# Earlier loads, one rounding step on ScalarE and a read-out with priority in a three-stage kernel (gated linear attention, softplus layer, routed experts)

## The chip, the cores and the metric

The kernel runs on one core of a Trainium2 chip. The metric is device time in microseconds (us) of one launch; the time shown for the kernel before is the median of 3 runs. One more execution was taken by the hardware profiler; its trace gives the rows below. Engines are called as in the profile: PE is TensorE (PEld its weight loads), DVE is VectorE, ACT is ScalarE, POOL is GpSimd, SP is the queue of SyncE that issues most transfers.

## The reference, cut to what matters

```
# attention: 4 batches, 8 heads, 768 positions, width 48
f = 1 / (1 + exp(-f_logit))
state = f[t][:, None] * state + outer(k[t], v[t]);  y[t] = q[t] @ state
x = y laid out as 3072 tokens of 384
# layer: w_in 384 x 2048, w_out 2048 x 384
h = x @ w_in;  g = max(h, 0) + log1p(exp(-abs(h)));  x2 = g @ w_out
# experts: 8, one per token (argmax), w1 384 x 1024, w2 1024 x 384
logits = x2 @ w_gate + modality_bias[modality_id];  e = argmax(logits)
out = softmax(logits)[e] * (max(x2 @ w1[e], 0) @ w2[e])
```

w_in and w_out come as 64-bit floats and are turned into 32-bit ones on the chip.

## The kernel before, in words

**Attention** is cut into 32 units (two heads, 384 positions each). A unit u has loads f, k, q, v (`att_load`), a preparation on ACT and DVE (`att_prep1`, `att_prep2`: 1 + exp(-f), a running product by a scan, its inverse, scaled keys and queries), transposes, products and masks on PE and DVE, and an output y on ACT (`att_out`) that SP copies into `xf` (`xf<-y`, 2 or 3 transfers per unit). Four units make one group of 384 tokens. Units 0 to 3 have a start of their own, `start_load` and `start_units`, where PE, DVE and ACT follow an order written out by hand (`manual_schedule`) and two units share one tile, so that pair 0 holds units 0 and 1 and pair 1 units 2 and 3. Every other order is the planner's: it takes the instructions of an engine by readiness and by a priority that falls in the order of the program.

**Layer.** For 8 groups G and 16 blocks i of 128 hidden columns, step s = 16 G + i does `up` (h in PSUM), softplus and `down` (adds into three PSUM tiles `x2ps`, one per 128 tokens). In group 0 (`softplus` with `lean`) the weights are 32-bit and are decoded while the steps run: `raw(n)` is a tile of 768 KB of raw words, even n for input weights, odd n for output weights; `scale_hi` is one ACT instruction on it, `decode` three DVE instructions (L461, L464, L465). From step 16 on each product is made of three (xh with wih, xl with wih, xh with wil; and so for w_out). For steps 16 to 111 two steps share one softplus, `pair` (48 of them): ACT makes exp (L626) and log (L627), DVE the rounding term w = ((e + 1) - 1) - e (L628, L629), the sum (L630), and after ACT's high part (L631) the low part (L632, L633).

**Read-out and routing.** After the last `down` of a group, `route1(G, j)` reads tile j of `x2ps` for the logits (L667) and the rows (ACT L672 for j = 0 and 2, DVE L670 for j = 1). The next group's first `down` writes the same three tiles, so it waits for them. `route2` picks the expert and POOL scatters the rows (L714). After the last group the experts run over slots of 256 or 128 tokens.

**Order at the start.** SP loads f and k of pair 0, f of pair 1, q of pair 0, two v, then the rest, then raw(0), raw(1), raw(2) and unit 4. f, k, q of unit 5 and raw(3) are held behind `marks["out"]`, the last transfer of unit 3's output (`follow`; `load_out(1)` with `first_out`). `NWARM` = 12 products with the identity run on PE in the start (L326) and 12 more at step 1 (L902); nothing reads their result.

Of the kernel before, what the change touches and what calls it, by code (L numbers as in the profile page):

```python
# [32 lines left out]
NWARM = 12  # L33
# [15 lines left out]
def moe_chain(ctx, tc, qT, kT, fT, vp, w_in, w_out, mod, w_gate, mbias, w1, w2, out):  # L49
# [40 lines left out]
    def att_load(u):  # L90
        d = units[u] = {}
        for nm, src in (("f", fT), ("k", kT), ("q", qT)):
            t = ap2.tile([128, TG], F32, tag=nm, name=nm, bufs=2 if nm == "f" else 3)
            ins = nc.sync.dma_start(t, src[u])
            if u == 5:
                follow(ins, marks["out"])
            d[nm] = t
        v = ap2.tile([128, 3 * 96], F32, tag="v", name="v", bufs=4)
        nc.sync.dma_start(v, vp[u])
        d["v"] = v  # L100
# [134 lines left out]
    def start_load():  # L235

        words = wih_raw.rearrange("p a b -> p (a b)").bitcast(F32)
        pair = [{nm: words[:, 768 * (4 * x + n):768 * (4 * x + n) + 768].rearrange("p (j t) -> p j t", j=2)
                 for n, nm in enumerate(("f", "k", "q", "F0"))} for x in range(2)]
        for u in range(4):  # L240
            units[u] = {nm: t[:, u % 2, :] for nm, t in pair[u // 2].items()}
        units["pairs"] = pair

        def get(nm, src, x):
            for j in range(2):
                nc.sync.dma_start(pair[x][nm][:, j, :], src[2 * x + j])

        def get_v(u):
            units[u]["v"] = ap2.tile([128, 3 * 96], F32, tag="v", name="v", bufs=4)
            nc.sync.dma_start(units[u]["v"], vp[u])  # L250

        get("f", fT, 0)
        get("k", kT, 0)
        get("f", fT, 1)
        get("q", qT, 0)
        get_v(0)
        get_v(1)
        get("k", kT, 1)
        get("q", qT, 1)
        get_v(2)  # L260
        get_v(3)

    def start_units():

        pair = units.pop("pairs")
        vec, act, pe = nc.vector, nc.scalar, nc.tensor
        h01 = [ps_h.tile([128, TG], F32, tag="h", name="h") for _ in range(2)]
        zu = x2ps[2]

        def scan(u):  # L270
            f = units[u]["f"]
            vec.tensor_tensor_scan(f, f, clampt.to_broadcast([128, TG]), 1.0, op0=ALU.mult, op1=ALU.min)

        def one_plus(u):
            f = units[u]["f"]
            act.activation(f, f, AF.Exp, scale=-1.0)
            act.activation(f, f, AF.Copy, bias=1.0)

        def keys(x):
            p = pair[x]  # L280
            vec.tensor_copy(fl[:, 2 * x:2 * x + 2], p["f"][:, :, TG - 1])
            vec.tensor_tensor(p["k"], p["k"], p["f"], op=ALU.mult)

        def inverse(x):
            p = pair[x]
            act.activation(p["F0"], p["f"], AF.Ln)
            act.activation(p["F0"], p["F0"], AF.Exp, scale=-1.0)

        def queries(x):
            p = pair[x]  # L290
            vec.tensor_tensor(p["f"], p["f"], p["F0"], op=ALU.mult)
            vec.scalar_tensor_tensor(p["F0"], p["f"], 2.0, p["F0"], op0=ALU.subtract, op1=ALU.mult)
            vec.tensor_tensor(p["q"], p["q"], p["F0"], op=ALU.mult)

        def sums(u):
            o = 144 * (u % 2)
            kt, v = units[u].pop("kt"), units[u]["v"]
            for c in range(3):
                for x in ([0, 2], [1, 2], [2])[c]:
                    for h in range(2):  # L300
                        vh = v[:, 96 * c + 48 * h:96 * c + 48 * h + 48]
                        n = 1
                        if x == 0:
                            n, vh = 2, vh.unsqueeze(1).to_broadcast([128, 2, 48])
                        pe.matmul(zu[64 * h:64 * h + 64, o + 48 * x:o + 48 * x + 48 * n], kt[:, c, 64 * h:64 * h + 64], vh,
                                  start=(u % 2 == 0 and c == 0 and x == 0), stop=True, skip_group_check=True)

        def states(u):
            o = 144 * (u % 2)
            for h in range(2):  # L310
                r, e = slice(64 * h, 64 * h + 64), slice(64 * h, 64 * h + D)
                act.copy(sts[u][r, 0:3, e], zu[r, o:o + 144].rearrange("p (c e) -> p c e", c=3))

        with tc.manual_schedule(engines={mybir.EngineType.PE, mybir.EngineType.DVE, mybir.EngineType.Activation}):
            for u in range(4):
                one_plus(u)
            scan(0)
            scan(1)
            keys(0)
            inverse(0)  # L320
            att_T(0)
            att_T(1)
            scan(2)
            scan(3)
            for _ in range(NWARM):
                pe.matmul(x2ps[0][:, 0:128], ident, ident, start=True, stop=True)  # L326
            inverse(1)
            sums(0)
            sums(1)
            queries(0)  # L330
            keys(1)
            att_A(0, h01)
            att_A(1, x2ps)
            states(0)
            states(1)
            att_T(2)
            att_T(3)
            queries(1)
            ya = ps_r.tile([128, 512], F32, tag="r", name="r")
            pa2 = [ps_r.tile([128, 512], F32, tag="r", name="r") for _ in range(2)]  # L340
            att_qS(0, ya)
            sums(2)
            sums(3)
            states(2)
            states(3)
            att_mask(0, h01)
            att_A(2, pa2)
            att_AV(0, ya)
            att_mask(1, x2ps)
            scale_hi(raw(0, 3))  # L350
            att_A(3, h01)
            att_out(0, ya)
            att_Y(1, x2ps[0])
            att_mask(2, pa2)
            att_out(1, x2ps[0])
            att_Y(2, x2ps[1])
            att_mask(3, h01)
            load_in(0, True)
            att_out(2, x2ps[1])
            scale_hi(raw(1, 2))  # L360
            yd = ps_r.tile([128, 512], F32, tag="r", name="r")
            att_Y(3, yd)
            att_out(3, yd)
            scale_hi(raw(2, 3))
        for u in range(4):
            units.pop(u)
# [100 lines left out]
    def raw(n, k):  # L467
        c = 1536 * (n % 4)
        return flat[n // 4 % 2][:, c:c + 1536].rearrange("p (k f) -> p k f", k=k)
# [148 lines left out]
    def pair(s):  # L618

        d = gst[s]  # L620
        e, r = d.pop("e"), d.pop("r")
        w = pp.tile([128, 2, TG], F32, tag="w2", name="w2", bufs=1)
        g = pp.tile([128, 2, TG], F32, tag="l2", name="l2", bufs=1)
        hi = pp.tile([128, 2, TG], F32R, tag="hi2", name="hi2")
        lo = pp.tile([128, 2, TG], F32R, tag="lo2", name="lo2")
        nc.scalar.activation(e, e, AF.Exp, scale=-1.0)  # L626
        nc.scalar.activation(g, e, AF.Ln, bias=1.0)  # L627
        nc.vector.tensor_scalar(w, e, 1.0, -1.0, op0=ALU.add, op1=ALU.add)  # L628
        nc.vector.tensor_tensor(w, w, e, op=ALU.subtract)  # L629
        nc.vector.tensor_tensor(g, r, g, op=ALU.add)  # L630
        nc.scalar.copy(hi, g)  # L631
        nc.vector.tensor_tensor(g, g, hi.bitcast(F32), op=ALU.subtract)  # L632
        nc.vector.tensor_tensor(lo, g, w, op=ALU.subtract)  # L633
        for j in range(2):
            gst[s + j]["hi"], gst[s + j]["lo"] = hi[:, j, :], lo[:, j, :]
# [27 lines left out]
    def route1(G, j):  # L663
        if j == 0:
            rt[G] = {"lg": sm("lg", [128, 3, 8]), "rows": gp.tile([128, 3, RW], F32, tag="rows", name="rows", bufs=1)}
        lg, rows = rt[G]["lg"], rt[G]["rows"]
        nc.vector.scalar_tensor_tensor(lg[:, j, :], x2ps[j][:, DM:DM + 8], 1.0 / WS, biasT[:, 3 * G + j, :],  # L667
                                       op0=ALU.mult, op1=ALU.add)
        if j == 1:
            nc.vector.tensor_scalar(rows[:, j, 0:DM], x2ps[j][:, 0:DM], 1.0 / WS, None, op0=ALU.mult)  # L670
        else:
            nc.scalar.activation(rows[:, j, 0:DM], x2ps[j][:, 0:DM], AF.Copy, scale=1.0 / WS)  # L672
# [169 lines left out]
    nc.sync.dma_start(raw(0, 3), src_in(0))  # L842
    nc.sync.dma_start(raw(1, 2), src_out(0))
    nc.sync.dma_start(raw(2, 3), src_in(1))
    att_load(4)
    late_consts()
    start_units()
    first_out = marks["out"]
    first_mask = marks["mask"]
    att_load(5)  # L850
    load_out(0, True)
    make_wp(0)
    load_in(1, True)

    at(0, lambda: load_out(1))
    at(5, pad_out)
    at(10, make_bias)
    for m in range(1, NF // 2):
# [433 lines left out]
```

## Time and profile before

| | |
|---|---|
| median of 3 runs | 841.43 us (839.96 to 841.88) |
| the profiled execution | 838.99 us |
| its span, first to last instruction | 837.2 us |
| PE busy in it | 801.8 us (96%) |
| DVE busy | 647.1 us (77%) |
| ACT busy | 536.5 us (64%) |

The profiled execution's own time is 1.8 us above its span; that part lies ahead of and behind the instructions. It stands 2.4 us under the median of the runs. Busy shares are means over stages with different limits, and ends of matmuls are modelled, so a busy PE is not PE at its peak.

### The profile page before, as it was taken

The page shows a single profiled execution, that of the slowest core. Times are in us where ns is not written, and L with a number is a line of the kernel's source. Part 1 is how long each engine was busy: PE and PEld are TensorE (multiplying, and loading weights), DVE is VectorE, ACT ScalarE, POOL GpSimd, SP SyncE. Part 2 cuts the span into 40 slices and gives each one's busy share as a digit, 9 for nine tenths or more (in the row PEclk, how much of TensorE's full clock was granted, in tenths as well). Part 3 has the DMA queues.
Part 4 walks back from the last instruction along what each step waited for, and adds up shares of the span by engine and source line. Part 5 has one row for each costly group of instructions (what it writes and reads, how often), then busy time and mean ns, then how long its engine had stood idle before and what let it go on. Part 6 is the DMA issues. An engine that isn't in the chain of part 4 may idle for free. (4 is left out here: it accounts for less than half of the span.)

```text
span 837.2 us, 15948 instructions
## 1 busy us (share of the span) xinstructions
PE 801.8 (96%) x5815; PEld 742.9 (89%) x5815; DVE 647.1 (77%) x1275; ACT 536.5 (64%) x1074; POOL 63.2 (8%) x79
## 2 busy tenths in 40 slices
PE   6799999999999999999999999999999999999995
PEld 5556668999999999899999999999999999999995
DVE  6899999988888888878887877888966666554441
ACT  6678787767667666667666665566756555555441
POOL 2000000200000010010010010101111110111100
PEclk9999999999999999999999999999999999999998
DMA  8685221321122132121221010199987667775590
GB/s 277 215 302 178 67 69 43 95 63 52 56 81 58 47 92 60 44 90 52 59 73 43 16 36 8 53 332 357 301 272 229 207 195 219 223 251 191 187 325 15
DMA packets 58522, 115.83 MB, mean 138 GB/s; under 512 B 7719, under 2 KB 33114, under 8 KB 58432
## 3 DMA queue, kind: packets, MB, share of 16 engines
q1 hardware_dynamic: 54144, 104.76, 39.4%
q0 software_dynamic: 3328, 9.49, 3.0%
q8 instruction: 49, 0.80, 0.4%
q10 hardware_dynamic: 960, 0.44, 0.2%
q14 instruction: 41, 0.34, 0.1%
HBM read 92.11 MB, written 18.62 MB: 132 GB/s over the span
## 5 line engine op out<-in xcount | busy, mean ns | idle before, releaser
L646 PE MATMUL x2ps<-woh,hi 128*128 128x392 f32 x336 | 115.5, 344 | 3.9 <-DVE rows L670 2.2
L566 PE MATMUL h<-xh,wih 128*128 128x384 f32 x336 | 118.1, 351 | 1.1 <-DVE e L580 0.7
L566 PE MATMUL h<-xl,wih 128*128 128x384 f32 x336 | 112.6, 335 | 2.2 <-DVE xl L393 2.2
L646 PE MATMUL x2ps<-woh,lo 128*128 128x392 f32 x336 | 114.3, 341 | 0.4 <-DVE lo L606 0.4
L646 PE MATMUL x2ps<-wol,hi 128*128 128x392 f32 x336 | 114.6, 341 | 0.0
L566 PE MATMUL h<-xh,wil 128*128 128x384 f32 x336 | 113.2, 337 | 0.0
L993 PE MATMUL h<-thl,w1h 128*128 128x256 f32 x576 | 106.5, 285 | 1.7 <-DVE hl L996 1.5
L993 PEld LDWEIGHTS h<-thl,w1h 128*128 128x128 f32 x576 | 89.2, 189 | 3.1 <-DVE hl L996 2.3
L955 DVE TENSOR_TENSOR w2l<-raw,w2h 128x768 fp32r<-128x768 f32 x64 | 60.7, 950 | 33.4 <-ACT w2h L954 33.1
L955 DVE TENSOR_TENSOR w1l<-raw,w1h 128x768 fp32r<-128x768 f32 x48 | 45.8, 954 | 48.7 <-ACT w1h L954 45.7
L993 PE MATMUL h<-thl,w1l 128*128 128x256 f32 x288 | 80.4, 281 | 0.0
L631 ACT CAST hi<-l 128x768 fp32r<-128x768 f32 x48 | 40.0, 834 | 62.0 <-DVE l L630 50.8
L1016 PE MATMUL x2ps<-w2h,hh 128*128 128x384 f32 x224 | 76.4, 341 | 0.0
L1016 PE MATMUL x2ps<-w2l,hh 128*128 128x384 f32 x224 | 75.1, 335 | 0.0
L954 ACT CAST w1h<-raw 128x768 fp32r<-128x768 f32 x48 | 40.1, 836 | 54.2 <-DMA raw<-in_w_dram 51.0
L1016 PE MATMUL x2ps<-w2h,hl 128*128 128x384 f32 x224 | 74.8, 336 | 0.0
L646 PEld LDWEIGHTS x2ps<-woh,hi 128*128 128x128 f32 x336 | 63.0, 188 | 6.4 <-DVE rows L670 3.5
L714 POOL DMA_INDIRECT xs<-rows,pos x24 | 26.7, 1111 | 552.9 <-ACT r L616 180.3
L566 PEld LDWEIGHTS h<-xh,wih 128*128 128x128 f32 x336 | 63.0, 188 | 5.4 <-DVE e L580 1.5
L566 PEld LDWEIGHTS h<-xl,wih 128*128 128x128 f32 x336 | 63.1, 188 | 3.5 <-DVE xl L393 3.5
L646 PEld LDWEIGHTS x2ps<-woh,lo 128*128 128x128 f32 x336 | 63.1, 188 | 1.1 <-DVE lo L606 1.0
L646 PEld LDWEIGHTS x2ps<-wol,hi 128*128 128x128 f32 x336 | 63.1, 188 | 0.0
(242 smaller groups left out, 1841.6 us busy)
## 6 DMA issues: line engine op xcount, KB each, us to landing
raw<-in_w_dram SPq DMA_DIRECT2D x112, 384.0 KB, 5.4
xs<-padt SPq DMA_DIRECT2D x8, 970.0 KB, 8.4
w1h<-in_w_dram SPq DMA_DIRECT2D x16, 384.0 KB, 6.1
f<-in_f_dram SPq DMA_DIRECT2D x28, 192.0 KB, 2.4
k<-in_k_dram SPq DMA_DIRECT2D x28, 192.0 KB, 2.6
q<-in_q_dram SPq DMA_DIRECT2D x28, 192.0 KB, 2.4
xr<-xs SPq DMA_DIRECT2D x12, 388.0 KB, 3.0
v<-in_v_dram SPq DMA_DIRECT2D x32, 144.0 KB, 2.3
```

The costliest lines, as they stand in the source:

```text
L566: nc.tensor.matmul(hp, w, x, start=(n == 0), stop=(n == len(terms) - 1))
L631: nc.scalar.copy(hi, g)
L646: nc.tensor.matmul(x2ps[j][:, 0:DM + 8], g[:, ts], w, start=(i == 0 and n == 0), stop=(i == NF - 1 and n == len(terms) - 1))
L714: ins = nc.gpsimd.indirect_dma_start(out=xs, out_offset=bass.IndirectOffsetOnAxis(ap=pos[:, j:j + 1], axis=0), in_=rows[:, j, :], in_offse ...
L954: nc.scalar.copy(hi[:, c], t)
L955: nc.vector.tensor_tensor(lo[:, c], t, hi[:, c].bitcast(F32), op=ALU.subtract)
L993: nc.tensor.matmul(hp[:, 0:SLOT], w[:, kd, fs], t[:, x, kd, :], start=(n == 0), stop=(n == 8))
L1016: nc.tensor.matmul(acc[:, 0:DM], g[:, f, ts], w[:, f, :], start=(f == 0 and n == 0), stop=(f == NF2 - 1 and n == 2))
```

## The change

- `start_load` loads f of pair 1 ahead of k of pair 0. In `start_units` DVE does all four scans before the keys of pair 0, and PE does 6 instead of 12 products with the identity.
- raw(3) is loaded right behind raw(2), ahead of unit 4, and scaled by ACT before step 0; `load_out(1)` only decodes it. Unit 5 is loaded right behind unit 4; its f, k and q are no longer held behind unit 3's output.
- In `pair` the first half of the rounding term, e + 1, is an ACT copy with a bias; DVE does (w - 1) - e as one instruction, behind the sum g = r + log.
- The instructions of `route1` are issued with a raised priority (offset 2000).

```
-            ins = nc.sync.dma_start(t, src[u])
-            if u == 5:
-                follow(ins, marks["out"])
+            nc.sync.dma_start(t, src[u])
...
         get("f", fT, 0)
+        get("f", fT, 1)
         get("k", kT, 0)
-        get("f", fT, 1)
...
-            scan(0)
-            scan(1)
+            for u in range(4):
+                scan(u)
             keys(0)
             inverse(0)
             att_T(0)
             att_T(1)
-            scan(2)
-            scan(3)
-            for _ in range(NWARM):
+            for _ in range(NWARM // 2):
...
-        nc.vector.tensor_scalar(w, e, 1.0, -1.0, op0=ALU.add, op1=ALU.add)
-        nc.vector.tensor_tensor(w, w, e, op=ALU.subtract)
+        nc.scalar.activation(w, e, AF.Copy, bias=1.0)
         nc.vector.tensor_tensor(g, r, g, op=ALU.add)
+        nc.vector.scalar_tensor_tensor(w, w, 1.0, e, op0=ALU.subtract, op1=ALU.subtract)
...
+        with tc.high_priority(offset=2000):
+            read_out(G, j, lg, rows)
+
+    def read_out(G, j, lg, rows):
         nc.vector.scalar_tensor_tensor(lg[:, j, :], x2ps[j][:, DM:DM + 8], 1.0 / WS, biasT[:, 3 * G + j, :],
...
     nc.sync.dma_start(raw(2, 3), src_in(1))
+    nc.sync.dma_start(raw(3, 2), src_out(1))
     att_load(4)
+    att_load(5)
     late_consts()
     start_units()
     first_out = marks["out"]
     first_mask = marks["mask"]
-    att_load(5)
     load_out(0, True)
     make_wp(0)
     load_in(1, True)
 
-    at(0, lambda: load_out(1))
+    scale_hi(raw(3, 2))
+    at(0, lambda: load_out(1, True))
```

## Rows read from the trace of the kernel before

**Rows 1.** Stretch, length, busy PE, PEld, DVE, ACT, POOL; clock, DMA share, GB/s.

```profile
42.00:130.00 88.00, 86.48 (x530) 54.84 (x529) 85.35 (x166) 71.42 (x155) 0.00 (x0) 0.99 0.45 146
130.00:160.00 30.00, 28.87 (x222) 26.15 (x221) 29.65 (x67) 21.77 (x46) 3.35 (x2) 1.00 0.24 74
160.00:560.00 400.00, 393.94 (x2884) 378.39 (x2883) 332.85 (x676) 263.19 (x528) 20.36 (x19) 1.00 0.22 66
```

**Rows 2.** What PE waited for from 160 to 560 us: total, times, longest.

```profile
PE x2ps L646 <- DVE rows L670: 2.2, 4, 0.8
PE h L566 <- DVE xl L393: 2.2, 4, 0.8
```

**Rows 3.** DVE in order of time, 20 to 47 us; in brackets idle time and releaser.

```profile
28.86 1.02 DVE L109 TENSOR_TENSOR_SCAN f<-f,fl,clampt 128x384 f32<-128x384 f32 x1
...
32.71 0.28 DVE L534 COPY ws<-r 64x128 f32<-64x128 f32 x1 [0.58 <-PE r L531]
...
34.09 1.02 DVE L109 TENSOR_TENSOR_SCAN f<-f,fl,clampt 128x384 f32<-128x384 f32 x1 [0.64 <-ACT f L108]
...
37.40 0.56 DVE L461 TENSOR_SCALAR wof<-woh_raw 128x768 int32<-128x768 int32 x1 [0.84 <-DMA woh_raw<-in_w_out_dram]
...
39.36 0.55 DVE L580 SCALAR_TENSOR_TENSOR e<-h,e 128x384 f32<-128x384 f32 x1
```

**Rows 4.** ACT in order of time, 20 to 47 us.

```profile
26.17 0.49 ACT L226 ACTIVATE y<-r 112x384 f32<-112x384 f32 x1 [0.69 <-DMA xf<-y]
26.56 0.93 ACT L445 ACTIVATE woh_raw<-woh_raw 128x768 f32<-128x768 f32 x1
...
37.40 0.91 ACT L445 ACTIVATE woh_raw<-woh_raw 128x768 f32<-128x768 f32 x1 [0.92 <-DMA woh_raw<-in_w_out_dram]
```

**Rows 5.** SP's issues in order of time, 0 to 60 us.

```profile
14.89 0.57 SPq L94 DMA_DIRECT2D q<-in_q_dram  x1
20.98 0.33 SPq L99 DMA_DIRECT2D v<-in_v_dram  x1
21.93 1.27 SPq L232 DMA_DIRECT2D xf<-y  x2
...
30.28 0.58 SPq L94 DMA_DIRECT2D f<-in_f_dram  x1
...
31.89 0.43 SPq L454 DMA_DIRECT2D woh_raw<-in_w_out_dram  x1
```

**Rows 6.** Stretches of 10 us, columns as in the first group.

```profile
10.00:20.00 10.00, 10.00 (x153) 9.39 (x152) 9.11 (x13) 6.13 (x15) 0.00 (x0) 1.00 0.98 339
20.00:30.00 10.00, 8.91 (x111) 7.75 (x110) 8.01 (x14) 5.97 (x12) 0.00 (x0) 1.00 0.38 114
```

**Rows 7.** Unit 0's output, issued from 21.5 to 23.25 us: KB each, us to landing.

```profile
xf<-y SPq DMA_DIRECT2D x2, 72.0 KB, 3.9
```

**Rows 8.** DVE at the start.

```profile
7.11 0.96 DVE L282 TENSOR_TENSOR wih_raw<-wih_raw 128x768 f32<-128x768 f32 x1
8.67 1.93 DVE L272 TENSOR_TENSOR_SCAN wih_raw<-wih_raw,clampt 128x384 f32<-128x384 f32 x2 [0.61 <-ACT wih_raw L277]
```

**Rows 9.** PE at the start.

```profile
9.47 4.19 PE L326 MATMUL x2ps<-ident 128*128 128x128 f32 x24
13.60 1.47 PE L305 MATMUL x2ps<-v,kt 128*64 128x96 f32 x40
```

**Rows 10.** Instructions of the paired softplus, 160 to 560 us: busy, mean ns, idle before.

```profile
L631 ACT CAST hi<-l 128x768 fp32r<-128x768 f32 x45 | 37.5, 834 | 60.8 <-DVE l L630 49.7 <-DVE run L698 8.8 <-DVE mx L711 2.3
L627 ACT ACTIVATE l<-e 128x768 f32<-128x768 f32 x44 | 37.2, 845 | 1.5 <-DVE rows L709 1.2
L628 DVE TENSOR_SCALAR w<-e 128x768 f32<-128x768 f32 x44 | 24.6, 559 | 17.6 <-ACT e L626 16.8
```

**Rows 11.** DVE at the end of a group, 398 to 408 us.

```profile
403.15 0.16 DVE L667 SCALAR_TENSOR_TENSOR lg<-x2ps,biasT 128x8 f32<-128x8 f32 x1
...
405.02 0.55 DVE L670 TENSOR_SCALAR rows<-x2ps 128x384 f32<-128x384 f32 x1
```

## Prediction

> **What bounds the kernel now.** I read the stretches first. From 160 to 560 us PE is busy 393.9 of 400 us, while DVE has 332.9 and ACT 263.2: the layer's groups 1 to 7 run at PE's pace. From 130 to 160 us DVE is busy 29.65 of 30 and PE 28.87; from 42 to 130 us both are nearly full, DVE 85.35 and PE 86.48 of 88 [rows 1]. So an edit in group 0 pays only by what it takes from DVE's idle time ahead of that stretch or from DVE's work in it, and an edit in groups 1 to 7 only by what PE waits for.
>
> Next the waits. Of PE's idle 6.1 us from 160 to 560 us, 2.2 us ended with the row read-out of tile 1 (L670, four times) and 2.2 us with xl (L393, four times) [rows 2]. Then the start, engine by engine. DVE's idle times between 30 and 38 us are 0.58 (waiting for PE), 0.64 (for unit 5's f, through ACT) and 0.84 us (for raw(3)) [rows 3]; ACT waits 0.92 us for raw(3) as well, and works 0.91 us on its scaling before it can go on with step 0's softplus [rows 4]. raw(3) was issued at 31.89 us and unit 5 at 30.28, both behind the outputs of units 0 to 3 [rows 5]. A span of 118 us that DVE fills begins right there, so each of these waits pushes all of group 0.
>
> **The change part by part.**
>
> *Loads.* raw(3) and unit 5's f, k, q leave the queue behind 30.28 us and go where SP has room: it issues nothing from 15.46 (14.89 + 0.57) to 20.98 us [rows 5]. Four issues move, of about 0.4 to 0.6 us each; the outputs of units 0 to 3 no longer stand ahead of them. With the data there, the three idle times on DVE can go: 0.58 + 0.64 + 0.84 = 2.06 us [rows 3]. The 0.58 us wait for PE goes too only if raw(3)'s decode stands ready to fill it; I count it, and without it the term is 1.48. raw(3)'s ACT instruction of 0.91 us is moved, not added. The next raw tiles and unit 6, which were issued behind these four, come about 2 us sooner; nothing at the end of this stretch waits for them.
>
> What it costs: the transfers are 768 KB and 3 x 192 KB, 1,376 thousand bytes, which at the 339 GB/s of 10 to 20 us are 4.1 us of transfer. That stretch is full (share 0.98); the next has room (0.38) [rows 6]. So the backlog that ended near 20 us ends near 24.1. Unit 0's output, issued at 21.93 us [rows 5], stood 3.9 us in this queue until it landed [rows 7]. It now has up to 24.1 - 21.93 = 2.2 us more in front of it, or the full 4.1 if the slowest of the 16 engines is as late as its 3.9 us suggests. ACT's y of unit 3 waits for just this transfer (0.69 us at 26.17), and behind it on ACT stand raw(2)'s scaling and unit 4's preparation [rows 4], which DVE's scan at 28.86 needs [rows 3]. DVE has other work meanwhile: the first decode instruction of raw(2) and of raw(3), which read the low words alone, 0.56 us each [rows 3]. I take 2.2 - 1.1 = +1.1 us; bounds 0 and +4.1.
>
> *Four scans first.* The keys of pair 0 stood at 7.11 us, ahead of the last two scans (1.93 us) [rows 8]. They now stand behind them, so PE's transposes, which need them, begin about 2 us later. PE gives back half of 4.19 us of identity products [rows 9], 2.1 us. Behind them the sums began at 13.60, the very moment the products ended [rows 9], so PE's chain from there to the masks moves with them. I take +0.1 us. Bounds: +2.2, if the six products that are dropped cost PE little because the six kept are the slow ones, and -0.6, the wait ahead of the two scans (0.61 us), if f's earlier landing ends it. The products are also what keeps PE busy before the sums; half of them keep it so for a shorter time.
>
> Start: -2.06 + 1.1 + 0.1 = -0.9 us.
>
> *Rounding term.* Per pair DVE loses L628, 0.559 us, and its second instruction keeps its size (two tensors, 768 columns). ACT gains one copy of 768 columns; the nearest row is L627 with 0.845 us [rows 10]. From 160 us on DVE's 0.559 us is worth nothing by itself, because PE sets the pace. ACT's 0.845 us falls where it now stands idle: ahead of L631 it waited 60.8 us over 45 pairs, 1.35 us each, 49.7 of it for DVE's sum [rows 10]. The sum now comes right behind the log, and the copy runs beside it. I take 0. Without that cover it is 0.845 us at each of 48 pairs, 40.6 us of ACT, of which only what PE waits for would show. Four pairs lie before 160 us, where DVE is full: 4 x 0.559 = 2.2 us of DVE's work goes. PE's own idle time from 130 to 160 us is 30 - 28.87 = 1.1 us [rows 1], and PE can't close up by more: -1.1 us, bounds 0 and -2.2.
>
> *Read-out with priority.* At a group's end the logits of tile 1 were read at 403.15 us and the rows of the same tile at 405.02, so 1.7 us of softplus work stood between them [rows 11], with the tile already complete. With priority L670 follows L667 at once, and PE's 2.2 us at four group ends [rows 2] go, but for the rest of an instruction that already runs on DVE. I take -1.7; bounds 0 and -2.2. For the xl waits I count nothing: ACT's xh waits for a transfer before them; DVE's lighter load could take up to 2.2 us [rows 2], which is in the range.
>
> **Sum.** -0.9 - 1.1 - 1.7 = -3.7 us against the profiled execution's 838.99 (span 837.2): 835.3. That execution stands 2.4 us under the median of the runs, 841.43, so the forecast median is 837.7 us.
>
> **A rule against it.** The copy costs 0.845 us where the removed DVE instruction costs 0.559 [rows 10]; ACT in 160 to 560 us has a third of its time free [rows 1]. The Trainium skill, "ScalarE: Activation LUTs", section "Rules for kernel authors", says to do additions on VectorE rather than ScalarE. By that rule the 48 copies would add 0.29 us of engine time each, 13.7 us, and were ACT what PE waits for, the forecast would be 851.4 us in place of 837.7.
>
> **Rivals.**
>
> 1. *The early loads hold up the outputs.* Unit 0's output lands the full 4.1 us later, and ACT, DVE and the first step behind it. For it: the 3.9 us of [rows 7], and the full stretch of [rows 6]; ACT's row shows the wait already [rows 4]. Against: the engines' share of 0.38 just behind. Then the start is -2.06 + 0.1 + 4.1 = +2.1 and the whole 2.1 - 1.1 - 1.7 = -0.7: 840.7 us.
>
> 2. *The middle does not move.* The planner already takes the read-out as early as its own clock lets it, and the 2.2 us that DVE sheds before 160 us only become idle time there. For it: PE's 28.87 of 30 us [rows 1]. Against: 1.7 us of other work between two reads of one tile [rows 11]. Then -0.9 alone: 840.5 us.
>
> 3. *ACT's copy takes the place of the waits removed* (slower). ACT works in order; a copy ahead of y or xh at a group's start delays the chain from PE's output over ACT, the transfer, xh and xl to PE, which already ends in a PE wait at four groups [rows 2]. Price: 0.845 us at each of seven group starts, 5.9 us: -3.7 + 5.9 = +2.2, 843.6 us. It decides from about 5.4 us on, 3.7 + 1.7. Against: ACT's 1.35 us of idle time ahead of L631. The rule above is this case's extreme.
>
> **How the numbers follow.** The forecast gets 0.57, rival 1 0.17, rival 2 0.11, rival 3 0.15. About 0.2% (1.7 us) is what a measurement of this kernel can tell from no change. The forecast's case lies beyond it, rivals 1 and 2 within, rival 3 beyond it on the other side: faster 0.57, same 0.28, slower 0.15. The likeliest case's own range is 835.0 to 839.7: down to -6.4 with the larger bounds of the read-out (-2.2), the rounding term (-2.2) and a start with no collision (-2.0), up to -1.7. The range for 8 in 10 is 834.5 to 842.5; it takes in rivals 1 and 2 and part of 3.
>
> **What would show it.** Right: raw(3) and unit 5 issued before 21 us; no DVE or ACT wait for raw(3) near 37 us; L580 of step 0, at 39.36 us [rows 3], a microsecond or more sooner; L670 right behind L667; no PE wait on it; ACT's idle time ahead of L631 down by about 0.8 us per pair; DVE down by 48 x 0.56 = 27 us and ACT up by 41. Wrong: y of unit 3 later than 28 us, or the first up of step 0 finishing later than before (rival 1); PE waits that end with ACT's r, xh or y (rival 3); and a new order of the planner's in group 0 that costs DVE idle time at a place that no row of before shows, which would make the whole sum wrong.

## The result, and the profile after

The changed kernel takes 846.42 us (median of 7 runs, 845.00 to 849.73), the kernel before beside it 839.96 (7 runs): ratio 1.0090, interval 1.0064 to 1.0116. It is slower: +6.5 us, where -3.7 was forecast; the forecast time was 837.7 and the range ended at 842.5. The profiled execution took 845.90 us, its span 844.1.

The stretches of after, columns as in [rows 1]:

```profile
42.00:130.00 88.00, 84.90 (x523) 53.34 (x522) 85.32 (x166) 71.20 (x154) 0.00 (x0) 1.00 0.42 139
130.00:160.00 30.00, 29.11 (x226) 26.79 (x225) 29.68 (x66) 25.96 (x53) 5.67 (x3) 1.00 0.25 74
160.00:560.00 400.00, 390.30 (x2854) 372.88 (x2852) 308.68 (x623) 295.74 (x564) 21.63 (x19) 1.00 0.21 63
```

From 160 to 560 us PE is idle 9.7 us, 6.1 before [rows 1]. What it waited for there:

```profile
PE h L562 <- DVE xl L389: 3.9, 4, 1.1
PE h L562 <- ACT r L612: 2.9, 3, 1.7
PE x2ps L642 <- ACT rows L672: 0.9, 3, 0.6
PE h L562 <- ACT xh L388: 0.8, 1, 0.8
```

The read-out of tile 1 (L670), 2.2 us in [rows 2], is gone from the list; xl went from 2.2 to 3.9 us, and ACT's r, the second half of the softplus' input, from 0.3 to 2.9 us. The row of r before:

```profile
PE h L566 <- ACT r L616: 0.3, 1, 0.3
```

The read-out itself does what it should; DVE in order at the same group's end as [rows 11], the logits of tiles 0 and 1 in one row:

```profile
405.05 0.24 DVE L667 SCALAR_TENSOR_TENSOR lg<-x2ps,biasT 128x8 f32<-128x8 f32 x2
405.20 0.55 DVE L670 TENSOR_SCALAR rows<-x2ps 128x384 f32<-128x384 f32 x1
```

The paired softplus, 160 to 560 us, columns as in [rows 10]:

```profile
L625 DVE TENSOR_TENSOR l<-r,l 128x768 f32<-128x768 f32 x44 | 42.0, 954 | 29.0 <-ACT l L623 28.7
L627 ACT CAST hi<-l 128x768 fp32r<-128x768 f32 x44 | 36.8, 837 | 28.6 <-DVE l L625 27.5 <-PE h L562 0.7 <-PE r L693 0.3
L624 ACT ACTIVATE w<-e 128x768 f32<-128x768 f32 x44 | 36.7, 834 | 0.0
```

ACT's idle time ahead of the high part fell from 60.8 to 28.6 us, so 32.2 us of the copy's 36.7 lie in what went. Most of the cover of the forecast was there. The loss shows elsewhere: in the two small writes at the end of `route2`, token numbers into the row tile and zeros beside them (L708, L709; 0.17 and 0.06 us). Neither the diff nor a row of the prediction's sum has them. DVE in order after and then before, at the same place of group 5:

```profile
433.58 0.56 DVE L121 TENSOR_TENSOR q<-q,F 128x384 f32<-128x384 f32 x1
439.35 0.17 DVE L708 COPY rows<-ids 128x3 int32<-128x3 int32 x1 [5.20 <-DMA xs<-rows,pos]
439.46 0.06 DVE L709 MEMSET rows<- 128x6 f32 x1
439.61 0.56 DVE L389 TENSOR_TENSOR xl<-xf,xh 128x384 fp32r<-128x384 f32 x1
...
441.81 0.95 DVE L625 TENSOR_TENSOR l<-r,l 128x768 f32<-128x768 f32 x1
```

```profile
432.36 0.56 DVE L123 TENSOR_TENSOR q<-q,F 128x384 f32<-128x384 f32 x1
434.73 0.17 DVE L708 COPY rows<-ids 128x3 int32<-128x3 int32 x1 [1.81 <-DMA xs<-rows,pos]
434.84 0.06 DVE L709 MEMSET rows<- 128x6 f32 x1
435.00 0.56 DVE L393 TENSOR_TENSOR xl<-xf,xh 128x384 fp32r<-128x384 f32 x1
```

The tile `rows` has one buffer. L708 needs nothing of its own group, so the planner puts it a group ahead: it runs at 439.35, its group's logits are read some 30 us later. But it has to wait until the group before has been scattered out of the tile, three scatters on POOL one after another. DVE works in order, and behind L708 stand xl, the keys, the sum. POOL after and before:

```profile
428.67 1.48 POOL L714 DMA_INDIRECT xs<-rows,pos  x1 [59.57 <-ACT l L623]
432.18 0.98 POOL L714 DMA_INDIRECT xs<-rows,pos  x1 [2.04 <-DMA xs<-rows,pos]
436.63 0.98 POOL L714 DMA_INDIRECT xs<-rows,pos  x1 [3.47 <-ACT F L113]
```

```profile
425.35 0.98 POOL L714 DMA_INDIRECT xs<-rows,pos  x1 [57.18 <-ACT e L626]
428.41 1.11 POOL L714 DMA_INDIRECT xs<-rows,pos  x1 [2.09 <-DMA xs<-rows,pos]
431.98 0.98 POOL L714 DMA_INDIRECT xs<-rows,pos  x1 [2.46 <-DMA xs<-rows,pos]
```

The last scatter is 4.65 us later than before, DVE's arrival (the end of q) 1.2 us, so the wait grew from 1.81 to 5.20 us. The first scatter is 3.32 us later, and that is DVE's own doing: it needs the row numbers `pos` that DVE writes (L705), here after and then before:

```profile
427.35 0.17 DVE L705 TENSOR_SCALAR pos<-m 128x3 int32<-128x3 f32 x1
```

```profile
424.03 0.16 DVE L705 TENSOR_SCALAR pos<-m 128x3 int32<-128x3 f32 x1
```

The scatter starts 1.2 us behind the end of this write in both traces, and 0.8 to 1.2 us behind it in groups 1 to 6 of both; the ACT instructions in its brackets are not what it goes by. Of the 3.32 us, 1.9 were there when the group's last logits were read (407.38 us, 405.49 before); the rest is the new order on DVE, where a scan (1.01 us) and a low part (0.94 us) now stand among the steps of the routing.

From the wait at L708 the chain runs over ACT, which waits for the sum, to PE (after):

```profile
442.80 0.83 ACT L627 CAST hi<-l 128x768 fp32r<-128x768 f32 x1 [4.46 <-DVE l L625]
443.72 0.49 ACT L611 ACTIVATE e<-h 128x384 f32<-128x384 f32 x1
444.11 0.48 ACT L612 ACTIVATE r<-h 128x384 f32<-128x384 f32 x1
```

```profile
444.65 0.44 PE L562 MATMUL h<-xh,wih 128*128 128x384 f32 x1 [0.54 <-ACT r L612]
```

Over six groups DVE sat idle ahead of L708 as follows, before and then after (us, times):

```profile
  DMA xs<-rows,pos: 12.3, 5
  issue: 0.4, 1
```

```profile
  DMA xs<-rows,pos: 18.7, 5
  issue: 3.6, 1
```

12.7 us against 22.3: the wait is old, the change made it longer.

### The profile page after: what moved, and what is told of

Its sections match the earlier page's. It is cut to its first block, busy times and chain, and to the rows that moved or that the text cites. A ratio compares the mean times of both kernels' runs of the same rounds, so it can differ in the third digit from the quotient of the medians.

```text
span 844.1 us, 15889 instructions
## 1 busy us (share of the span) xinstructions
PE 802.2 (95%) x5803; PEld 741.8 (88%) x5803; DVE 626.7 (74%) x1227; ACT 577.9 (68%) x1122; POOL 67.7 (8%) x79
## 5 line engine op out<-in xcount | busy, mean ns | idle before, releaser
L957 DVE TENSOR_TENSOR w2l<-raw,w2h 128x768 fp32r<-128x768 f32 x64 | 60.8, 952 | 39.9 <-ACT w2h L956 39.9
L957 DVE TENSOR_TENSOR w1l<-raw,w1h 128x768 fp32r<-128x768 f32 x48 | 45.8, 954 | 41.4 <-ACT w1h L956 37.8
L714 POOL DMA_INDIRECT xs<-rows,pos x24 | 30.2, 1260 | 552.0 <-DVE l L625 143.9
L625 DVE TENSOR_TENSOR l<-r,l 128x768 f32<-128x768 f32 x48 | 45.8, 953 | 29.0 <-ACT l L623 28.7
```

The source lines that it names most:

```text
L714: ins = nc.gpsimd.indirect_dma_start(out=xs, out_offset=bass.IndirectOffsetOnAxis(ap=pos[:, j:j + 1], axis=0), in_=rows[:, j, :], in_offse ...
L957: nc.vector.tensor_tensor(lo[:, c], t, hi[:, c].bitcast(F32), op=ALU.subtract)
```

## The experiments

The theories were named in this order: A, the rounding term makes the loss (A1 by DVE's order, A2 by ACT's load); B, the priority; C, the start; then P, the priority of the last group costs time among the experts; and W, the wait at L708. All runs in one table. "Wait" is DVE's idle time ahead of the write of the token numbers and "PE idle" 400 less PE's busy time, both from 160 to 560 us; "layer" is when the last logits are read, so from there on the experts run. Traces are one execution each, times medians; ratios are to the kernel before on the same chip.

| run | what it is | time | ratio (interval) | wait | PE idle | layer |
|---|---|---|---|---|---|---|
| before | | 840.0 | 1 | 12.7 | 6.1 | 573.6 |
| e1 | rounding alone | 843.7 | 1.0040 (1.0017 to 1.0064) | 22.2 | 9.7 | 580.9 |
| e2 | priority alone | 841.5 | 1.0014 (0.9996 to 1.0031) | 9.1 | 2.3 | 570.0 |
| e3 | start alone | 837.3 | 0.9944 (0.9920 to 0.9968) | 9.8 | 4.9 | 574.5 |
| e4 | all but rounding | 839.8 | 0.9992 (0.9969 to 1.0016) | 10.3 | 3.2 | 568.9 |
| e5 | all, copy ahead of the log | 842.1 | 1.0026 (1.0005 to 1.0047) | 9.0 | 5.7 | 574.4 |
| e6 | e4, priority not for the last group | 837.3 | 0.9974 (0.9950 to 0.9997) | 11.7 | 3.9 | 570.2 |
| e7 | e4, a copy that nothing reads | 841.6 | 1.0020 (0.9999 to 1.0042) | 11.2 | 6.0 | 572.5 |
| e8 | e4, w - e behind the sum | 839.8 | 1.0013 (0.9989 to 1.0036) | 9.7 | 2.9 | 569.2 |
| e12 | after again | 847.5 | 1.0067 (1.0040 to 1.0093) | 22.7 | 9.4 | 578.6 |
| e9 | after, writes on POOL | 833.6 | 0.9908 (0.9884 to 0.9931) | none | 2.7 | 563.5 |
| e10 | e6, writes on POOL | 833.0 | 0.9905 (0.9884 to 0.9926) | none | 0.9 | 565.7 |
| e11 | e6 with rounding, writes on POOL | 832.2 | 0.9891 (0.9866 to 0.9916) | none | 0.9 | 565.4 |
| e13 | before, writes on POOL | 835.7 | 0.9948 (0.9925 to 0.9971) | none | 1.4 | 567.8 |
| e14 | e1, writes on POOL | 836.9 | 0.9977 (0.9957 to 0.9997) | none | 1.8 | 567.8 |
| e15 | after, writes held back on DVE | 833.6 | 0.9928 (0.9902 to 0.9954) | 0 | 3.3 | 569.6 |
| e16 | e3, writes on POOL | 837.3 | 0.9964 (0.9947 to 0.9982) | none | 1.3 | 566.9 |

**The change in its parts.** e1, e2 and e3 each put one part into the kernel before; e4 takes the rounding term out of the changed one:

```
# e1, in pair
-        nc.vector.tensor_scalar(w, e, 1.0, -1.0, op0=ALU.add, op1=ALU.add)
-        nc.vector.tensor_tensor(w, w, e, op=ALU.subtract)
+        nc.scalar.activation(w, e, AF.Copy, bias=1.0)
         nc.vector.tensor_tensor(g, r, g, op=ALU.add)
+        nc.vector.scalar_tensor_tensor(w, w, 1.0, e, op0=ALU.subtract, op1=ALU.subtract)
# e2, in route1
+        with tc.high_priority(offset=2000):
+            read_out(G, j, lg, rows)
...
# e3: the hunks of start_load, start_units, att_load and the loads; e4: after less e1
```

> The kernel before with only the rounding term of the paired softplus changed (copy on ACT, one DVE instruction behind the sum). Theory A: this edit alone makes the loss, because one more DVE instruction of 0.95 us now lies behind the log, so masks, queries, keys and xl come later at group starts: 5 to 7 us slower than the kernel before, PE idle time from 160 to 560 us up by about 5 us, its waits on ACT's r and on xl. Theory B, the read-out's priority or the planner's new order makes the loss, and theory C, the start's loads make it: this kernel within 1 us of the kernel before.

> The kernel before with only the raised priority of the read-out. Theory A: 1 to 2 us faster than the kernel before, since the four PE waits on the read-out of tile 1 (2.2 us) go. Theory B: 3 us or more slower, since the read-out pushes softplus work or masks of the next group back. Theory C: 0 to 2 us faster.

> The kernel before with only the edits of the start: raw(3) and unit 5 loaded early, f of pair 1 ahead of k of pair 0, four scans first, half of the identity products. Theory A: 1 to 2 us faster, as the progress of PE at 240 us in the changed kernel (1.35 us ahead) says, and that lead kept to the end. Theory B: the same. Theory C: 3 us or more slower, with the loss behind 240 us, since unit 4 to 6 and all later loads stand elsewhere in the queue.

> The changed kernel with the old rounding term put back (two DVE instructions ahead of the sum, no copy on ACT). Theory A: 2 to 4 us faster than the kernel before, 8 to 10 us faster than the changed one. Theory B or C: still 4 us or more slower than the kernel before.

e1 is slower, by 3.5 us where 5 to 7 were expected, and its layer ends 7.3 us later; against e4 the changed kernel's ends 8.5 later. So the rounding term makes the loss, as theory A has it. B fails: the priority alone takes PE's idle time from 6.1 to 2.3 us, more than forecast, and the layer ends 3.6 us sooner; but the time stays. C fails too: the start alone is faster, by 2.9 us in the medians. That e4 is no faster than the kernel before was not expected: something takes the gains back behind the layer.

**How the rounding term does it, and what takes the priority's gain.** e5 and e8 change DVE's order, e7 ACT's load, e6 the priority:

```
# e5: after, ACT's copy between exp and log, DVE's instruction ahead of the sum
# e8: e4 with
+        nc.vector.tensor_tensor(g, r, g, op=ALU.add)
         nc.vector.tensor_tensor(w, w, e, op=ALU.subtract)
-        nc.vector.tensor_tensor(g, r, g, op=ALU.add)
# e7: e4 with
         nc.scalar.copy(hi, g)
+        nc.scalar.activation(e, e, AF.Copy, bias=1.0)
# e6: e4 with
+        with tc.high_priority(offset=2000 if G < NG - 1 else 0):
```

> The changed kernel with ACT's copy made between exp and log, and DVE's one instruction for the rounding term ahead of the sum, so that behind the log DVE has the sum and two instructions, as in the kernel before. Theory A1, the DVE instruction that stands behind the log makes the loss in the layer: 3 to 6 us faster than the changed kernel, about 841 to 843. Theory A2, the 0.85 us of ACT per pair make it, since ACT takes its work in order and the log comes that much later here: within 1.5 us of the changed kernel, or slower.

> The changed kernel with the old rounding term, and the priority of the read-out for groups 0 to 6 only, not for the last group. Theory P: the priority wins some 3 to 4 us in the layer, and that of the last group loses as much behind it, because ACT's scaling of the first expert slot's output falls behind three instructions that wait for the second slot's weights, so the stores, SP's next slot and its weights come late (PE idle 3.4 us near 612 us). Then this kernel is 3 to 4 us faster than the same kernel with the priority everywhere, about 836, and that idle time is gone. Rival: the transfers of the expert weights (0.9 of the DMA engines' time there) set the pace there, whatever the order; then it stays at about 839.5.

> The changed kernel with the old rounding term on DVE, and one more ACT copy per pair, of the size of the rounding copy and behind the log, whose result nothing reads: ACT's load without the new dependence. Theory A2 (ACT's load in order makes the loss): about as slow as the changed kernel, 844 to 848. Theory A1 (the DVE instruction behind the log makes it): within 1.5 us of the same kernel without the copy, 838.5 to 841.

> The changed kernel with both instructions of the rounding term on DVE and no copy on ACT, but the second one, w - e, behind the sum instead of ahead of it: the new order on DVE without ACT's load. Theory A1 (one more DVE instruction of 0.95 us behind the log): 4 to 7 us slower than the same kernel with the old order, 844 to 847. Theory A2 (ACT's load): within 1.5 us of it, 838.5 to 841.

A1 fails: e8 has the new order and ends the layer 0.3 us behind e4, though e5's 842.1 us are what A1 said. A2 holds in part: e7's copy puts the layer's end 3.6 us later, not 8.5, and its 841.6 us lie between what A1 and A2 said. e5 lies between, 5.5 us behind e4. No one piece is the loss; in e1 and after (and e12) alone the wait at L708 is 22 us, and that gave theory W.

P shows in the order of ACT. In e2 both of the first expert slot's scalings (L1024) stand behind three instructions that wait for PE, and the store behind them; later PE waits:

```profile
592.20 0.94 ACT L999 ACTIVATE hh<-h 128x256 fp32r<-128x256 f32 x3 [2.31 <-PE h L997]
593.00 1.07 ACT L1024 ACTIVATE o<-x2ps,xr 128x384 f32<-128x384 f32 x2
```

```profile
615.22 0.38 PE L997 MATMUL h<-thl,w1h 128*128 128x256 f32 x1 [3.63 <-DVE hl L1000]
```

Before and in e6 the same scaling stands ahead of these, the one before and the other in e6:

```profile
589.06 0.58 ACT L1020 ACTIVATE o<-x2ps,xr 128x384 f32<-128x384 f32 x1 [0.81 <-PE x2ps L1016]
```

```profile
586.01 0.58 ACT L1022 ACTIVATE o<-x2ps,xr 128x384 f32<-128x384 f32 x1
```

In e6 PE's longest wait up to 640 us is 1.6 us, and by medians it is 2.4 us faster than e4, less than the 3 to 4 expected; the intervals overlap. That the order on ACT makes e2's wait is argued, not shown: SP loads the next slot's rows at 603.40 us in e2 and at 602.85 in e6, only 0.55 us apart. The rival has a share: e13, e14 and e16, without any priority, have the same wait, 5.7 (row below, e13), 5.9 and 7.1 us. The end of the layer alone does not set it either: the layers of e10 and e11 end sooner than that of e13, and PE's longest wait there is 2.4 and 2.1 us.

```profile
PE h L993 <- DVE hl L996: 5.7, 1, 5.7
```

Such a wait has a second price, in TensorE's clock. In e2, behind the 3.63 us, the granted clock is 0.66 from 615 to 620 us, so a part of that stretch ran at the lower of its two levels (1.2 GHz): two products of L997 take 0.63 us from 617.22 us on, 0.40 at 615.68. From 600 to 640 us the granted clock is 1.00 in the four traces whose longest PE wait from 560 to 640 us is 1.6 us at most (before, e1, e3, e6). It is lower in 12 of the 14 with 2.1 us or more: 0.96 in after, e2, e4, e10, e11 and e12, 0.91 in e7, e9 and e13 to e16. Worked out from these shares, 40 us at 0.96 lose 1.6 us of PE's work at full clock and 40 us at 0.91 lose 3.6; both are estimates.

**The wait.** Two ways to take it from DVE: the writes go to POOL, where the scatters stand anyway (e9, e10, e11), or they stay on DVE but behind their own group's logits (e15). A second buffer for the tile was not tried.

```
# e9, e10, e11, e13, e14, e16, in route2
-        nc.vector.tensor_copy(rows.bitcast(I32)[:, :, 385], ids[:, 3 * G:3 * G + 3])
-        nc.vector.memset(rows[:, :, 386:388], 0.0)
+        nc.gpsimd.tensor_copy(rows.bitcast(I32)[:, :, 385], ids[:, 3 * G:3 * G + 3])
+        nc.gpsimd.memset(rows[:, :, 386:388], 0.0)
# e15
-        nc.vector.tensor_tensor(lg, lg, bc(mx), op=ALU.subtract)
+        sub = nc.vector.tensor_tensor(lg, lg, bc(mx), op=ALU.subtract).ins
...
+        follow(nc.vector.tensor_copy(rows.bitcast(I32)[:, :, 385], ids[:, 3 * G:3 * G + 3]), sub)
+        follow(nc.vector.memset(rows[:, :, 386:388], 0.0), sub)
# e12: no edit
```

> The changed kernel with the two small writes of the next group's row tile (token numbers, zeros) on POOL instead of DVE. On DVE the first of them waits, in order, until the last scatter of the group before has landed: 22 us over six groups in the changed kernel, 10 us in the same kernel with the old rounding term. Theory W: this wait holds up the sum, and behind it ACT and PE, at pairs 13, 21, 29 and 37; without it the layer ends 4 to 6 us sooner, total 840 to 842.5. Rival (theory A2, ACT's load alone, and no such wait): within 1.5 us of the changed kernel.

> The start as changed, the priority for groups 0 to 6 only, the old rounding term, and the two small writes on POOL. Theory W: the 12 us that DVE waits there in the kernel without the move cost PE some of its 4 us of idle time in the layer, so 1 to 3 us faster than that kernel, 834 to 836.5. Rival: with the old rounding term the wait is hidden; then 837.3 as there.

> All edits of the change, the rounding copy on ACT too, but the priority not for the last group and the two small writes on POOL. Theories P and W together: 846.4 less 3 to 4 and less 4 to 6, so 837 to 839.5, no slower than the kernel before. Rival (the copy's load on ACT is the whole loss): 842 or more.

> The changed kernel itself, beside the other three on one chip. All theories: 0.8 to 1.1% slower than the kernel before, about 847; if it is much less, the differences from it that the other runs were read by shrink with it.

e9 beside e12 on one chip: 833.6 against 847.5, 13.9 us, more than twice what was expected. PE's waits in e9, 160 to 560 us; no xl and no r among them:

```profile
PE x2ps L642 <- ACT hi L601: 1.2, 2, 1.0
PE x2ps L642 <- ACT rows L672: 0.6, 1, 0.6
PE x2ps L642 <- DVE lo L602: 0.4, 1, 0.4
PE h L562 <- DVE e L576: 0.2, 1, 0.2
```

And the sum still waits for the log there as in the changed kernel, only ACT's high part no longer waits so long for it (e9):

```profile
L625 DVE TENSOR_TENSOR l<-r,l 128x768 f32<-128x768 f32 x44 | 42.1, 956 | 31.3 <-ACT l L623 31.1
L627 ACT CAST hi<-l 128x768 fp32r<-128x768 f32 x44 | 36.9, 839 | 13.6 <-DVE l L625 11.8 <-issue 0.7 <-PE r L150 0.7
```

So DVE's new wait for the log is not what makes the loss; the old wait for the scatter is. e11, the whole change without that wait and without the last group's priority, is the fastest by median, 832.2 us, and beats both kernels (e9, e10 and e11 have overlapping intervals); e10, the same without the rounding copy, is level with it.

**What stayed open then.**

> The kernel before with the two small row writes on POOL, nothing of the change. Theory W: the 12.7 us that DVE waits there in it cost PE some of its 6 us of idle time in the layer: 2 to 5 us faster than the kernel before. Rival: in the kernel before the wait is covered, and only the rounding copy made it matter: within 1 us of the kernel before.

> The kernel before with the rounding term on ACT as changed, and the two small writes on POOL. Theory W: with the wait gone the copy costs nothing, as the prediction had it: within 1.5 us of the kernel with the writes on POOL alone. Theory A2, ACT's load costs 3 to 4 us by itself (as the copy that nothing reads did): 2.5 us or more slower than that kernel.

> The changed kernel with the two small writes still on DVE, but held in its order behind their own group's logits, so that they can't stand a group ahead and wait for the last scatter. Theory W (the wait in order): as fast as with the writes on POOL, 832 to 836. Rival (DVE is relieved of the instructions, or POOL's order is what gains): within 3 us of the changed kernel, 844 to 848.

> The edits of the start alone, with the two small writes on POOL. If the start gains 2 to 4 us by itself, as the run of it alone said, this is 2 to 4 us faster than the kernel before with the writes on POOL; if that gain came from a shift of the same wait, the two agree within 1 us.

e15 keeps the two writes on DVE and comes to 833.6 us: it is the wait in DVE's order, not the engine. Its trace is of its slowest execution, 838.9 us, so its layer and PE's idle time are not those of the median. Its row of the writes names no idle time any more, and its first is at 208.7 us, where group 1's logits are read, in place of 164.9:

```profile
L708 DVE COPY rows<-ids x6: 160/161/163, 208.7 to 517.2; 128x3 int32<-128x3 int32 x6
```

e13: the kernel before carried 4.3 us of it. e14 against e13: layers end at the same 567.8 us, times 1.2 us apart by medians, 2.4 by ratios, with overlapping intervals, and e11 with the copy is 0.8 us faster than e10 without it; so with the wait gone the copy costs nothing that these runs can tell. e16 is not faster than e13 but 1.6 us slower, with overlapping intervals, though e3 is faster than the kernel before; what the start is worth in the end is not settled.

## Why the prediction was wrong

**The start, -0.9, and -1.1 ahead of 160 us.** The number comes out near, but not as the work of these two terms. The last logits of group 0 are read at 131.7 to 138.5 us in the 13 traces with the start's edits, mean 134.9, and at 136.3 to 138.1 in the 5 without, mean 137.2: 2.4 us, forecast 2.0. But the two with the start's edits alone, e3 and e16, have 138.5 and 136.6, no sooner than those without; the other eleven have the priority too, which moves these very reads. And PE's idle time from 130 to 160 us, which was to give the 1.1, went from 1.1 to 0.9 us. So the agreement may be luck. What the start's edits do in every trace is this: PE's wait for step 0's sum is 1.2 to 1.4 us in the 13 and 4.5 to 5.7 in the 5, and the granted clock from 40 to 60 us is 1.00 in the 13 and 0.84 to 0.92 in the 5. No term of the sum held either.

In the parts: raw(3) was issued at 12.00 us, but unit 5's f did not go into SP's gap; SP waits on to 20.49 us, and f goes behind:

```profile
20.49 0.33 SPq L97 DMA_DIRECT2D v<-in_v_dram  x1
20.86 0.43 SPq L94 DMA_DIRECT2D f<-in_f_dram  x1
```

The early data also made two new waits, in ACT's order at the start, one for raw(3) and one for unit 5's f:

```profile
22.58 0.96 ACT L441 ACTIVATE woh_raw<-woh_raw 128x768 f32<-128x768 f32 x1 [1.17 <-DMA woh_raw<-in_w_out_dram]
...
25.17 0.52 ACT L103 ACTIVATE f<-f 128x384 f32<-128x384 f32 x1 [1.27 <-DMA f<-in_f_dram]
```

Behind them stand a scaling at 26.53 us, for which DVE waits 2.07, and y of unit 3, 1.2 us later than in [rows 4]; the first up is at 29.37, PE idle 2.02 ahead of it. Of DVE's three idle times [rows 3] the last two are gone, the one for PE grew from 0.58 to 1.03; step 0's sum stands at 38.65 us, 0.7 sooner, where a microsecond was forecast. The 1.2 us are close to the 1.1 that the term held, bounds 0 to 4.1, but that is luck: the term had y wait for unit 0's output, and no row of y names that transfer any more. The sign set for rival 1, a later first up, came true (ACT first reads its result at 35.55 us, 33.97 before), its price of 4.1 us did not: step 0's sum stands sooner, not later.

**The read-out, -1.7.** The priority does in the layer what was forecast, and more: PE's wait on L670 is gone and e2's layer ends 3.6 us sooner. But the priority is not the only way to end that wait. In e13, without any priority and with the two writes off DVE, PE waits for neither L670 nor xl any more, the two waits of [rows 2] (160 to 560 us, all rows):

```profile
PE x2ps L646 <- ACT rows L672: 0.7, 1, 0.7
PE x2ps L646 <- DVE lo L606: 0.4, 1, 0.4
PE x2ps L646 <- ACT hi L605: 0.3, 1, 0.3
```

So the prediction's 1.7 us of other work between two reads were not the whole reason for it. e2's time did not move, since the experts behind it gave it back, in PE's wait there and the lower clock behind it; no term of the sum went on past 560 us.

**The rounding term: "I take 0".** This is the step that failed. Its two reasons, the sum right behind the log and the copy beside it, hold in the main: ACT's idle time ahead of the high part fell by 0.70 us per pair (60.8 / 45 less 28.6 / 44; forecast 0.8), and e14 and e11 show no clear cost once the wait is gone. In place of 0 the term measured 3.5 us alone (e1) and 6 to 8 us beside the other parts (e4 against after and e12). What the step left out is that the same edit moves everything else on ACT, DVE and POOL, and that at each group's end DVE stands in its order before a scatter that it can't pass. I went from PE's waits, on L670 and xl, to the engines that ended them and stopped there; what held xl up in its turn, the L708 just ahead of it, I did not ask, although [rows 10] names its neighbour L709. ACT's busy time rose by 41.4 us as forecast (577.9 against 536.5), DVE's fell by 20.4, forecast 27.

**The sum.** The wait cost the changed kernel 13.9 us (e12 to e9) and the kernel before 4.3 (e13): 9.6 us more. Without it the change is worth 833.6 - 835.7 = -2.1 us by medians, by ratios (0.9908 against 0.9948) -3.4; e15 against e13, on one chip, gives -2.2 and -1.7, with overlapping intervals. The forecast was -3.7. So one wait that the sum did not hold turned the sign, and without it sign and rough size come back. The single terms are not shown by that: without the wait neither the start (e16 against e13) nor the rounding term (e14) is faster by itself, and the priority was not run alone there.

**The rivals.** Rival 3 had the sign, its mechanism not quite: the wait is DVE's for POOL's scatter, and ACT's load alone (e7) costs 3.6 us of the layer and some 2 us of time (e4's interval overlaps), within its 5.9. Rival 2 fails: the middle moved, both ways. The new order of the planner that the prediction feared in group 0 came at every group's end instead. The rule of the Trainium skill, "ScalarE: Activation LUTs", section "Rules for kernel authors", that additions belong on VectorE would by the prediction's working have given 851.4 us. Once the wait at L708 is gone, e11 with the copies and e10 without are level, so no run here bears it out as a cost of time of its own.

**What stays open.** Why the second and third scatter came further apart (7.96 us from the first to the third, 6.63 before). What the start is worth by itself. And the whole size: the layers of after and e9 end at 577.4 and 563.5 us, 13.9 apart; 2.3 of it lie ahead of the end of group 0, where the traces with start and priority differ by as much as 131.7 to 136.6 us, and PE's idle time shows 7.0; ends of matmuls are modelled, and the rest can't be placed.

## What to carry to other kernels

Follow a wait back until it ends at work that is really bound: ask of the late instruction which one stood ahead of it in the order of its engine, and what that one waited for. A short instruction that needs only a free buffer may be put far ahead by a planner and then block its engine until a slow reader has let the buffer go; hold it behind its own group, or give it to the engine that waits for that reader anyway. And a gain in one stage counts only if the next stage can start earlier, so the sum has to go on to the end of the program.

## What the runs showed of the hardware

In groups 0 to 6 a group's three scatters of 128 rows go one by one: POOL sat idle 1.9 to 4.2 us between them in the changed kernel, in 9 of 14 rows until the one before had landed, so a tile stays taken for 9 to 11 us (428.67 to 439.35 us after, 425.35 to 434.73 before). This is how the program orders them: for the last group it declares that they don't depend on each other, and there POOL sat idle 0.3 us between them (584.31, 585.59 and 586.87 us after). The same for all groups was not run. An indirect store took POOL about 1 to 1.7 us in most rows, 4.5 us once in each of e10 and e11, 6.2 in e6 and 9.4 in each of e13, e14 and e16, while the second expert slot's weights were loading. TensorE's granted clock fell behind PE's long waits among the experts (0.66 from 615 to 620 us in e2, behind 3.63 us) and stayed at 1.00 in all four traces without one, but also in two with one (e5 and e8).
